# Reordering a layer norm, attention and gMLP kernel on one core: roots moved from GpSimd to ScalarE, v weights read strided, q/k before z2

## The chip, the cores and the metric

The kernel runs on one core of a Trainium2 chip. The metric is device time in microseconds (us), the median of several executions. The engines are named as the profile names them: PE (TensorE matmul; PEld is its weight load), DVE (VectorE), ACT (ScalarE), POOL (GpSimd), SP (SyncE, which issues most of the DMAs).

## The reference, cut to what matters

```python
xn = layernorm(x)                                  # x: 2048 x 512, bf16
# A: local attention, 32 heads of 16, window of 8 keys at distance 0, 2, .., 14
q, k, v = heads(xn @ wqkv)
o = softmax(q . k[t - 2w] * 16**-0.5) applied to v[t - 2w];  A = o @ wo
# B: gMLP
z = gelu(xn @ w_in)                                # 2048 x 1376, halves z1 and z2
g = w_sp @ layernorm(z2) + b_sp                    # 2048 x 2048 times 2048 x 688
B = (z1 * g) @ w_out
out = x + A + B
```

## The kernel before

The 16 row tiles of 128 are handled in four blocks of four tiles: block j holds tiles j, 4+j, 8+j, 12+j. Every tile is normalised on DVE, transposed (blocks 0 and 1 by PE and a ScalarE copy, blocks 2 and 3 by a DMA that transposes), and then used as one side of all projections. The q/k products (a shifted elementwise multiply on DVE, 1.15 us for each 128x2048) feed `logits`, a matmul that sums over a head's 16 dimensions. After that come the gate matmuls `g_mm` (w_sp times z2), which need every z2 tile.

In two waits of the kernel before's trace the engine did not pass over the instruction that had to wait. DVE stands idle for 3.06 us in front of block 3's normalisations, though the inputs of the two products written behind them were complete (ACT's copy of block 1's last q/k group ends at 32.31 us); those products start at 42.30 us. PE stands idle for 2.73 us in front of the last quarter of the first logits, with 16 q/k matmuls of block 2, whose tiles had been in use since 33.70 us, written behind it; they start at 43.95 us. The root of the layer norm is taken in three ways:

```python
def rsqrt(E, y, v, s):                 # a bit trick and three Newton steps: 15 small operations
    h, a = nwt[:, 0, s], nwt[:, 1, s]
    E.tensor_scalar(h, v, EPS, None, ALU.add)
    E.tensor_scalar(y.bitcast(I32), h.bitcast(I32), -0.5, float(0x5f3759df), ALU.mult, ALU.add)
    E.tensor_scalar(h, h, -0.5, None, ALU.mult)
    for _ in range(3):
        E.tensor_tensor(a, y, y, ALU.mult)
        E.tensor_tensor(a, a, h, ALU.mult)
        E.tensor_scalar(a, a, 1.5, None, ALU.add)
        E.tensor_tensor(y, a, y, ALU.mult)
```

Block 0 uses a ScalarE square root for each tile, block 1 and z2 use `rsqrt` on DVE, blocks 2 and 3 use `rsqrt` on GpSimd. The first part of the body, with cuts:

```python
# ... block 0: statistics, ScalarE root, normalise, transpose; z2 of two tiles as well ...
ln_block(V, 1)                         # statistics and rsqrt on DVE
for i in blk(1): ln_apply(i)
ln_block(G, 2)                         # statistics on DVE, rsqrt on GpSimd
for c in range(C):
    qk_mm(0, c)                        # ... block 1's transpositions in between
for i in blk(3): ln_stats(i)
ln_block_apply(2)                      # DVE normalises, SP issues the transposing DMA
ln_rstd(G, slice(3, NT, 4))            # rsqrt of block 3 on GpSimd
for c in range(C):
    qk_mm(1, c)
    if c == 3: ln_block_apply(3)
    prod_c(0, c); prod_c(1, c)         # DVE products of the first two groups
    if c == 1: z2s(0, 2)
for k in range(C):                     # v weights regrouped: 16 dims x 32 heads
    G.tensor_copy(wv_r[:, k], wv[:, k, :].rearrange("p (h d) -> p d h", d=DH))
qk_mm(2, 0); qk_mm(2, 1); z2s(0, 3)
logits(0)
# ... q/k of blocks 2 and 3, then z2, v and logits alternately ...
```

`v_mm` is one v group: 32 matmuls, each with a weight tile of 32 columns out of `wv_r` and a stream of 512 columns. `z2s` is one z2 tile: eight matmuls, gelu on ScalarE, and a sum of squares on ScalarE.

Of the kernel before, what the change touches and what calls it, by code (L numbers as in the profile page):

```python
# [8 lines left out]
F32 = mybir.dt.float32  # L9
# [10 lines left out]
TB = 4  # L20
# [28 lines left out]
def kernel(  # L49
# [32 lines left out]
    vp = r_x[:].rearrange("p (d t) -> p d t", d=DH)  # L82
    r_w = sb.tile([P, 8192], BF16, name="r_w")
    wqk = r_w[:, 0:4096].rearrange("p (k f) -> p k f", k=C)
    wv = r_w[:, 4096:6144].rearrange("p (k f) -> p k f", k=C)
    wv_r = r_w[:, 6144:8192].rearrange("p (k d h) -> p k d h", k=C, d=DH)
    a_sb = r_w[:, 0:4096].rearrange("p (w t) -> p w t", w=W)
    wout = r_w[:, 4096:4096 + MCH * D].rearrange("p (m n) -> p m n", m=MCH)
    r_qk = sb.tile([P, 2 * C * (HALO + S)], BF16, name="r_qk")
# [33 lines left out]
    zvar = sb.tile([P, NT], F32, name="zvar")  # L123
    zrstd = sb.tile([P, NT], F32, name="zrstd")
    eps_t = sb.tile([P, 1], F32, name="eps_t")
    nwt = sb.tile([P, 2, NT], F32, name="nwt")


    def load_x0(E, tb):
# [2 lines left out]
    def load_wqk(E, h):  # L132

        w = wqk.rearrange("p k (s c f) -> p k s c f", s=2, c=C)
        src = A_wqkv[:, 0:2 * D].rearrange("(k p) (s c f) -> p k s c f", p=P, s=2, c=C)
        for s in range(2):
            E.dma_start(w[:, :, s, 2 * h:2 * h + 2, :], src[:, :, s, 2 * h:2 * h + 2, :])
# [2 lines left out]
    load_x0(A, 2)  # L140
    load_x0(SP, 1)
    load_x0(A, 3)
    SP.dma_start(w_z2[:], B_w_in[:, FH:F].rearrange("(k p) f -> p k f", p=P))
    load_wqk(A, 0)
    SP.dma_start(xall[:, 1], xblk[1])
    load_wqk(SP, 1)
    for j in range(2, 4):
        SP.dma_start(xall[:, j], xblk[j])
    SP.dma_start(w_z1[:], B_w_in[:, 0:FH].rearrange("(k p) f -> p k f", p=P))
    SP.dma_start(wv, A_wqkv[:, 2 * D:3 * D].rearrange("(k p) f -> p k f", p=P))  # L150
    SP.dma_start(b16[:], B_b_sp.rearrange("(j p) -> j p", p=P))


# [19 lines left out]
    def ln_stats(i):  # L173
        j, tb = i % 4, i // 4
        V.bn_stats(stats[:, i, :], xall[:, j, tb, :])  # L175
        V.bn_aggr(mv[:, i, :], stats[:, i, :])  # L176

    def rsqrt(E, y, v, s):

        h, a = nwt[:, 0, s], nwt[:, 1, s]  # L180
        E.tensor_scalar(h, v, EPS, None, ALU.add)
        E.tensor_scalar(y.bitcast(I32), h.bitcast(I32), -0.5, float(0x5f3759df), ALU.mult, ALU.add)
        E.tensor_scalar(h, h, -0.5, None, ALU.mult)
        for _ in range(3):
            E.tensor_tensor(a, y, y, ALU.mult)
            E.tensor_tensor(a, a, h, ALU.mult)  # L186
            E.tensor_scalar(a, a, 1.5, None, ALU.add)  # L187
            E.tensor_tensor(y, a, y, ALU.mult)  # L188

    def ln_rstd(E, sl):  # L190
        rsqrt(E, rstd[:, sl], mv[:, sl, 1], sl)

    def ln_sqrt(i):
        A.activation(rstd[:, i:i + 1], mv[:, i:i + 1, 1], ACT.Sqrt, bias=eps_t[:])

    def ln_recip(i):
        V.reciprocal(rstd[:, i:i + 1], rstd[:, i:i + 1])

    def ln_apply(i):
        j, tb = i % 4, i // 4  # L200
        V.tensor_scalar(xall[:, j, tb, :], xall[:, j, tb, :], mv[:, i, 0:1], rstd[:, i:i + 1],  # L201
                        ALU.subtract, ALU.mult)

    def tr(i):
        j, tb = i % 4, i // 4
        pt = ps_aux.tile([P, C, P], BF16, name="pt", tag="aux")
        for c in range(C):
            PE.transpose(pt[:, c, :], xall[:, j, tb, c * P:(c + 1) * P], ident[:])
        return pt

    def tr_copy(i, pt):
        A.copy(xnT[:, :, i * P:(i + 1) * P], pt[:])

    def tr_dma(i):
        j, tb = i % 4, i // 4
        SP.dma_start_transpose(xnT[:, :, i * P:(i + 1) * P], xall[:, j, tb, :])

    def zmm(i, wz):
        pz = ps_mm.tile([P, 2, TBS], F32, name="pz", tag="mm")
        for hh in range(2):  # L220
            for kc in range(C):
                PE.matmul(pz[:, hh, 0:FHALF], xnT[:, kc, i * P:(i + 1) * P],  # L222
                          wz[:, kc, hh * FHALF:(hh + 1) * FHALF], start=(kc == 0), stop=(kc == C - 1))
        return pz
# [8 lines left out]
        junk = work.tile([P, FH], BF16, name="junk", bufs=1)  # L233
        A.activation(junk[:], z2[:, i, :], ACT.Square, accum_out=zsq[:, q:q + 1])  # L234

    def z2_stat(s):
        V.tensor_scalar(zmean[:, s], zsum[:, s], 1.0 / FH, None, ALU.mult)
        V.tensor_tensor(zm2[:, s], zmean[:, s], zmean[:, s], ALU.mult)
        V.tensor_scalar(zvar[:, s], zsq[:, s], 1.0 / FH, None, ALU.mult)
        V.tensor_tensor(zvar[:, s], zvar[:, s], zm2[:, s], ALU.subtract)  # L240
        rsqrt(V, zrstd[:, s], zvar[:, s], s)

    def z2_norm(i):
        q = 4 * (i % 4) + i // 4
        V.tensor_scalar(z2[:, i, :], z2[:, i, :], zmean[:, q:q + 1], zrstd[:, q:q + 1], ALU.subtract, ALU.mult)
# [71 lines left out]
    def v_mm(d2):  # L317
        pv = ps_mm.tile([P, 2, TBS], F32, name="pv", tag="mm")
        for dd in range(2):
            for kc in range(C):  # L320
                for tb in range(TB):
                    PE.matmul(pv[32 * tb:32 * tb + 32, dd, :], wv_r[:, kc, 2 * d2 + dd, :],  # L322
                              xnT[:, kc, tb * TBS:(tb + 1) * TBS],
                              start=(kc == 0), stop=(kc == C - 1), tile_position=(0, 32 * tb))
        A.copy(vp[:, 2 * d2:2 * d2 + 2, HALO:HALO + TBS], pv[:])
# [67 lines left out]


    pwm = ps_aux.tile([P, TBS], F32, name="pwm", tag="aux")
    for _ in range(9):
        PE.matmul(pwm[:], warm[:, 0:P], warm[:], start=True, stop=True)

    def blk(j):
        return [4 * tb + j for tb in range(TB)]  # L400

    def ln_block(E, j):
        for i in blk(j):
            ln_stats(i)
        ln_rstd(E, slice(j, NT, 4))

    def ln_block_apply(j):
        for i in blk(j):
            ln_apply(i)
            tr_dma(i)  # L410

    def z2_fin(*js):

        z2_stat(slice(4 * js[0], 4 * js[-1] + 4))
        for j in js:
            for i in blk(j):
                z2_norm(i)

    def z2s(j, tb):
        i = blk(j)[tb]  # L420
        z2_gelu(i, zmm(i, w_z2))
        z2_sq(i)

    def prods(g):
        for ww in range(4):
            prod_w(g, ww)

    t0 = blk(0)
    ln_stats(t0[0])
    ln_sqrt(t0[0])  # L430
    ln_stats(t0[1])
    ln_sqrt(t0[1])
    ln_recip(t0[0])
    ln_apply(t0[0])
    pt0 = tr(t0[0])
    tr_copy(t0[0], pt0)
    ln_stats(t0[2])
    ln_sqrt(t0[2])
    ln_recip(t0[1])
    ln_apply(t0[1])  # L440
    pt1 = tr(t0[1])
    tr_copy(t0[1], pt1)
    ln_stats(t0[3])
    ln_sqrt(t0[3])
    ln_recip(t0[2])
    ln_apply(t0[2])
    pz0 = zmm(t0[0], w_z2)
    pt2 = tr(t0[2])
    tr_copy(t0[2], pt2)
    ln_recip(t0[3])  # L450
    ln_apply(t0[3])
    pt3 = tr(t0[3])
    tr_copy(t0[3], pt3)
    z2_gelu(t0[0], pz0)
    z2_gelu(t0[1], zmm(t0[1], w_z2))
    z2_sq(t0[0])
    ln_block(V, 1)
    for i in blk(1):
        ln_apply(i)
    ln_block(G, 2)  # L460
    for c in range(C):
        qk_mm(0, c)
        if c == 0:
            z2_sq(t0[1])
        if c >= 2:
            for i in blk(1)[2 * c - 4:2 * c - 2]:
                tr_copy(i, tr(i))
    for i in blk(3):
        ln_stats(i)
    ln_block_apply(2)  # L470
    ln_rstd(G, slice(3, NT, 4))
    for c in range(C):
        qk_mm(1, c)
        if c == 3:
            ln_block_apply(3)
        prod_c(0, c)
        prod_c(1, c)
        if c == 1:
            z2s(0, 2)
    for k in range(C):  # L480
        G.tensor_copy(wv_r[:, k], wv[:, k, :].rearrange("p (h d) -> p d h", d=DH))
    qk_mm(2, 0)
    qk_mm(2, 1)
    z2s(0, 3)
    logits(0)
    qk_mm(2, 2)
    qk_mm(2, 3)
    prods(2)
    logits(1)
    qk_mm(3, 0)  # L490
    qk_mm(3, 1)
    prods(3)
    z2s(1, 0)
    logits(2)
    qk_mm(3, 2)
    qk_mm(3, 3)
    prods(4)
    z2s(1, 1)
    logits(3)
    G.memset(vp[0:32, :, 0:HALO], 0.0)  # L500
    v_mm(0)
    z2s(1, 2)
    v_mm(1)
    z2s(1, 3)
    prods(5)
    sm_max(0)
    logits(4)
    z2s(2, 0)
    v_mm(2)
    z2s(2, 1)  # L510
    logits(5)
    v_mm(3)
    z2s(2, 2)
    prods(6)
    prods(7)
    pb = ps_aux.tile([P, NT], BF16, name="pb", tag="aux")
    PE.transpose(pb[:], b16[:], ident[0:NT, 0:NT])
    A.copy(b_col[:], pb[:])
    z2_fin(0, 1)
    z2s(2, 3)  # L520
    v_mm(4)
    z2s(3, 0)
    logits(6)
    z2s(3, 1)
    v_mm(5)
    logits(7)
    add_mask()
    sm_max(1)
    for n in range(NWSP):
        load_wsp(n)  # L530
    z2s(3, 2)
    z2s(3, 3)
    for n in range(4):
        z1_mm(n)
    z2_fin(2, 3)
    v_mm(6)
    v_mm(7)
    SP.dma_start(vp[32:P, :, 0:HALO], vp[0:P - 32, :, TBS:TBS + HALO])
    sm_exp(0)
    sm_exp(1)  # L540
# [54 lines left out]
```

## Time and profile before

| | before |
|---|---|
| median time (225.39 to 228.09, 4 runs) | 227.78 us |
| span of the profiled run | 225.5 us |
| PE busy from 9 to 54 us (45.0 us) | 38.20 us, granted clock 0.89 |
| PE busy from 54 to 97.25 us (43.25 us) | 43.19 us |
| PE busy from 97.25 us, the first gate matmul, to 221.5 us | all 124.25 us |

Busy time by stretch in the kernel before; in each line come the stretch, its length, the busy time (and the number of instructions) of PE, PEld, DVE, ACT and POOL, the granted PE clock, the DMA share and GB/s:

```profile
9.00:54.00 45.00, 38.20 (x204) 17.92 (x204) 31.82 (x63) 25.17 (x39) 18.01 (x35) 0.89 0.33 90
54.00:97.25 43.25, 43.19 (x496) 21.60 (x495) 40.89 (x70) 35.73 (x69) 0.29 (x1) 1.00 0.30 58
97.25:221.50 124.25, 124.25 (x962) 74.55 (x960) 102.18 (x115) 29.46 (x33) 0.24 (x1) 1.00 0.60 129
```

From 54 to 221.5 us PE is busy throughout, at a granted clock of 1.00, so only less PE work or a faster PE could shorten that part. The slack that the change is after lies in the 45 us from 9 to 54: almost 7 us of idle PE, and a granted clock of 0.89.

The next lines are the PE timeline of the kernel before in that stretch (start, duration of a run of like instructions, source line; in brackets the idle time before it and what ended it). L257 is q/k, L222 z2, L288 logits, L208 a transposition:

```profile
27.65 3.62 PE L257 MATMUL pq<-xnT,r_w 128*128 128x512 bf16 x16
33.70 5.21 PE L257 MATMUL pq<-xnT,r_w 128*128 128x512 bf16 x16 [2.44 <-DMA xnT<-r_x]
38.75 1.33 PE L222 MATMUL pz<-w_z_75,xnT 128*128 128x344 bf16 x8
40.01 0.83 PE L288 MATMUL pl<-r_pr,rsel 128*32 128x512 bf16 x12
43.57 0.45 PE L288 MATMUL pl<-r_pr,rsel 128*32 128x512 bf16 x4 [2.73 <-DVE r_pr L271]
43.95 5.22 PE L257 MATMUL pq<-xnT,r_w 128*128 128x512 bf16 x16
```

PE waits 2.44 us for block 2's transposing DMA and 2.73 us for a DVE product. After each of those waits the 16 q/k matmuls take 5.2 us; the same 16 take 3.62 us at 27.65. The trace shows a half clock there. The next two lines of the kernel before give a stretch behind the first wait and the one after it (stretch, length, PE's busy time and number of matmuls, granted clock, DMA share, GB/s):

```profile
33.55:36.96 3.41, 3.26 (x8) 0.50 0.00 0
37.10:38.70 1.60, 1.60 (x9) 1.00 0.00 0
```

The q/k matmuls start 0.43 us apart in the first and 0.22 us apart in the second. Two more such stretches of 3.41 us are recorded before the gate: from 43.79 us, behind the second wait, and from 9.65 us, over z2 matmuls. So these two waits are paid for twice, once in idle time (2.44 and 2.73 us) and once in slower matmuls (5.2 us for 16 instead of 3.62).

What the waits hang on is seen on DVE and POOL. The DVE timeline of the kernel before (L201 is the normalisation, L271 the product):

```profile
26.60 1.39 DVE L201 TENSOR_SCALAR r_x<-r_x,mv,rstd 128x512 bf16<-128x512 bf16 x4 [1.21 <-POOL rstd L188]
27.90 6.89 DVE L271 TENSOR_TENSOR r_pr<-r_qk 128x2048 bf16<-128x2048 bf16 x6
37.86 4.52 DVE L201 TENSOR_SCALAR r_x<-r_x,mv,rstd 128x512 bf16<-128x512 bf16 x4 [3.06 <-POOL rstd L188]
```

The POOL timeline of the kernel before (L186 is one multiply of the Newton step, L481 the copy of the v weights):

```profile
25.74 0.21 POOL L186 TENSOR_TENSOR nwt<-nwt 128x4 f32<-128x4 f32 x1
...
27.79 7.07 POOL L186 TENSOR_TENSOR nwt<-nwt 128x4 f32<-128x4 f32 x1
...
37.75 4.48 POOL L481 COPY r_w<-r_w 128x512 bf16<-128x512 bf16 x4
```

One 128x4 multiply that takes 0.21 us at 25.74 takes 7.07 us at 27.79: it is recorded from 0.11 us before the first of the six DVE products (27.90 us) until just after the last has ended (34.86 against 34.79 us). And four normalisations that take 1.39 us at 26.60 take 4.52 us at 37.86, beside the four GpSimd copies. The two engines get in each other's way here in both directions, and both victims were what the rest waited for.

### The profile page before, as it was taken

Reading aid. Unit: us, or ns where it says so; the run is one execution under the profiler, and the core shown is the slowest. Engines: PE = TensorE matmul, PEld = TensorE weight load, DVE = VectorE, ACT = ScalarE, POOL = GpSimd, SP = SyncE. Lnnn points to the kernel's source line nnn. Section 1 sums busy time; section 2 is a strip of 40 time slices with the busy share of each in tenths; the row PEclk is TensorE's granted clock in tenths of the full one; section 3 lists DMA queues with packets and bytes.
Section 4 is the critical chain, followed back from the end, with each engine's and each line's share of the span. In section 5 each row is a group of like instructions: output and inputs, shape, how many; then the busy total and the mean of one; then the engine's idle time right before and its main releaser. Section 6 shows DMA issues by size and latency. Waiting matters only on the chain.

```text
span 225.5 us, 4086 instructions
## 1 busy us (share of the span) xinstructions
PE 210.7 (93%) x1674; PEld 115.9 (51%) x1674; DVE 181.6 (81%) x267; ACT 93.8 (42%) x147; POOL 22.1 (10%) x55
## 2 busy tenths in 40 slices
PE   7597959599999999999999999999999999999992
PEld 2354424134444545556666665466665466664440
DVE  4589794909799999999999999989999298882412
ACT  3299452446788898785233221012221012221000
POOL 6000798400000000000000000000000000000000
PEclk9889997889999999999999999999999999999999
DMA  5991040400000009999974766999871341111142
GB/s 172 332 350 53 0 93 0 93 6 0 0 3 0 3 0 174 221 169 219 224 161 99 155 129 146 191 149 243 206 158 35 77 144 37 35 38 35 49 140 93
DMA packets 63410, 24.97 MB, mean 111 GB/s; under 512 B 52848, under 2 KB 63264, under 8 KB 63264
## 3 DMA queue, kind: packets, MB, share of 16 engines
q1 hardware_dynamic: 62048, 23.93, 47.2%
q10 hardware_dynamic: 1344, 0.79, 1.2%
q8 instruction: 13, 0.21, 0.4%
q14 instruction: 5, 0.04, 0.1%
HBM read 9.98 MB, written 2.10 MB: 54 GB/s over the span
## 4 chain that ended last, share of the span: by engine, by line
PE 76%; DVE 8%; POOL 6%; DMA 4%; issue 2%; SPq 1%; DVEq 1%; ACT 0%
PE pg L357 33%; PE pz L222 14%; PE po L387 9%; PE pv L322 6%; PE po L381 6%; DMA r_x<-in_A_x_dram 4%; PE pq L257 4%; POOL nwt L186 4%; PE pl L288 3%; DVE r_x L201 3%; DVE stats L175 2%; DVE r_pr L281 1%; DVE mv L176 1%; POOL nwt L187 1%; POOL rstd L188 1%
## 5 line engine op out<-in xcount | busy, mean ns | idle before, releaser
L357 PE MATMUL pg<-z_77,r_qk 128*128 128x344 bf16 x512 | 76.9, 309 | 0.0
L357 PEld LDWEIGHTS <-r_qk 128*128 128x128 bf16 x512 | 50.0, 98 | 25.0 <-issue 0.4
L333 DVE TENSOR_TENSOR r_pr<-r_x,r_w 128x2048 bf16<-128x2048 bf16 x32 | 38.2, 1220 | 0.3
L360 ACT ACTIVATE gs<-pg,b_col 128x688 bf16<-128x688 f32 x16 | 13.3, 833 | 56.5 <-PE pg L357 56.5
L257 PE MATMUL pq<-xnT,r_w 128*128 128x512 bf16 x128 | 32.1, 409 | 4.1 <-DMA xnT<-r_x 2.4
L222 PEld LDWEIGHTS <-xnT 128*128 128x128 bf16 x256 | 24.7, 100 | 17.9 <-issue 5.2
L337 DVE TENSOR_TENSOR r_pr<-r_pr 128x2048 bf16<-128x2048 bf16 x28 | 33.8, 1219 | 0.1
L281 DVE TENSOR_TENSOR r_pr<-r_qk 128x2048 bf16<-128x2048 bf16 x24 | 27.5, 1218 | 6.8 <-ACT r_qk L261 6.8
L391 DVE TENSOR_TENSOR r_qk<-po,r_qk 128x512 bf16<-128x512 f32 x16 | 10.3, 686 | 18.2 <-PE po L387 18.2
L222 PE MATMUL pz<-w_z_75,xnT 128*128 128x344 bf16 x128 | 22.5, 323 | 1.7 <-DMA w_z_75<-in_B_w_in_dram 1.7
L257 PEld LDWEIGHTS <-r_w 128*128 128x128 bf16 x128 | 12.9, 104 | 21.6 <-issue 10.1
L261 ACT CAST r_qk<-pq 128x1024 bf16<-128x1024 f32 x16 | 16.2, 1012 | 16.4 <-PE pq L257 16.4
L387 PE MATMUL po<-r_w,uT 128*128 128x512 bf16 x96 | 21.4, 379 | 0.0
L250 ACT ACTIVATE z1u<-pz 128x688 bf16<-128x688 f32 x16 | 11.8, 742 | 21.8 <-PE pz L222 21.8
L222 PE MATMUL pz<-w_z_76,xnT 128*128 128x344 bf16 x128 | 20.8, 309 | 0.0
L387 PEld LDWEIGHTS <-uT 128*128 128x128 bf16 x96 | 9.1, 98 | 12.1 <-issue 1.7
L322 PE MATMUL pv<-xnT,r_w 128*32 128x512 bf16 x256 | 15.1, 380 | 0.0
L381 PE MATMUL po<-r_lg,r_pr 32*128 32x512 bf16 x256 | 14.5, 375 | 0.0
L175 DVE BATCH_NORM_STATS2 stats<-r_x 128x6 f32<-128x512 bf16 x16 | 10.7, 669 | 4.7 <-DMA r_x<-in_A_x_dram 4.7
L228 ACT ACTIVATE z_77<-pz 128x688 bf16<-128x688 f32 x16 | 11.9, 742 | 2.4 <-PE pz L222 2.4
L234 ACT ACTIVATE junk<-z_77 128x688 bf16<-128x688 bf16 x16 | 12.4, 778 | 0.4
L201 DVE TENSOR_SCALAR r_x<-r_x,mv,rstd 128x512 bf16<-128x512 bf16 x16 | 8.9, 604 | 4.5 <-POOL rstd L188 4.3
(77 smaller groups left out, 150.3 us busy)
## 6 DMA issues: line engine op xcount, KB each, us to landing
r_lg<-in_A_wo_dram SPq DMA_DIRECT2D x4, 512.0 KB, 9.4
r_qk<-in_A_x_dram SPq DMA_DIRECT2D x16, 128.0 KB, 2.2
out_dram<-r_qk SPq DMA_DIRECT2D x16, 128.0 KB, 1.7
r_x<-in_A_x_dram SPq DMA_DIRECT2D x3, 512.0 KB, 9.2
w_z_75<-in_B_w_in_dram SPq DMA_DIRECT2D x1, 688.0 KB, 7.2
w_z_76<-in_B_w_in_dram SPq DMA_DIRECT2D x1, 688.0 KB, 8.6
r_w<-in_B_w_out_dram SPq DMA_DIRECT2D x1, 640.0 KB, 6.6
r_w<-in_A_wqkv_dram ACTq DMA_DIRECT2D x2, 256.0 KB, 8.5
```

The source lines that it names most:

```text
L175: V.bn_stats(stats[:, i, :], xall[:, j, tb, :])
L201: V.tensor_scalar(xall[:, j, tb, :], xall[:, j, tb, :], mv[:, i, 0:1], rstd[:, i:i + 1], ALU.subtract, ALU.mult)
L222: PE.matmul(pz[:, hh, 0:FHALF], xnT[:, kc, i * P:(i + 1) * P], wz[:, kc, hh * FHALF:(hh + 1) * FHALF], start=(kc == 0), stop=(kc == C - 1))
L257: PE.matmul(pq[:, s, :], wqk[:, kc, s * D + c * P:s * D + (c + 1) * P], xnT[:, kc, :].rearrange("p (b j t) -> p b j t", b=TB, j=4)[:, :, j ...
L261: A.copy(dst[:, :, :, j, :], pq[:].rearrange("p s (b t) -> p s b t", b=TB))
L281: V.tensor_tensor(pr[g % 2][:, :, ww], q4, k4, ALU.mult)
L322: PE.matmul(pv[32 * tb:32 * tb + 32, dd, :], wv_r[:, kc, 2 * d2 + dd, :], xnT[:, kc, tb * TBS:(tb + 1) * TBS], start=(kc == 0), stop=(kc = ...
L333: V.tensor_tensor(pw_t[n], vp[:, :, off:off + P], a_sb[:, slot_w(w), ts].unsqueeze(1).broadcast_to([P, DH, P]), ALU.mult)
L337: V.tensor_tensor(pw_t[n] if dst is None else dst, pw_t[n], pw_t[m], ALU.add)
L357: PE.matmul(pg[:, hh, 0:FHALF], wsp[n % NWSP][:, k, :], z2[:, k, hh * FHALF:(hh + 1) * FHALF], start=(q == 0), stop=(q == NT - 1))
L381: PE.matmul(pos[tb], op[32 * tb:32 * tb + 32, d, o * P:(o + 1) * P], wo_r[32 * tb:32 * tb + 32, d, :], start=(d == 0), stop=False, tile_po ...
L387: PE.matmul(pos[tb], uT[:, o % 2, m, tb * P:(tb + 1) * P], wout[:, m, :], start=False, stop=(m == MCH - 1))
```

## The change

Its intent is to have PE start on q/k as soon as four tiles are ready, to have no GpSimd arithmetic in the way of DVE, and to keep PE full until the gate. The diff, cut to its core (cuts marked with `...`):

```diff
-    wv = r_w[:, 4096:6144].rearrange("p (k f) -> p k f", k=C)
-    wv_r = r_w[:, 6144:8192].rearrange("p (k d h) -> p k d h", k=C, d=DH)
+    wv = r_w[:, 4096:6144].rearrange("p (k h d) -> p k d h", k=C, d=DH)
...
-    SP.dma_start(w_z2[:], ...)
-    load_wqk(A, 0)
-    SP.dma_start(xall[:, 1], xblk[1])
+    load_wqk(SP, 0)
+    A.dma_start(xall[:, 1], xblk[1])
     load_wqk(SP, 1)
     for j in range(2, 4):
         SP.dma_start(xall[:, j], xblk[j])
+    SP.dma_start(w_z2[:], ...)
...
-    def ln_rstd(E, sl):
-        rsqrt(E, rstd[:, sl], mv[:, sl, 1], sl)
+    def ln_sqrt(sl):
+        A.activation(rstd[:, sl], mv[:, sl, 1], ACT.Sqrt, bias=eps_t[:])
+    def ln_recip(sl):
+        V.reciprocal(rstd[:, sl], rstd[:, sl])
...  (z2: Newton steps on DVE for blocks 0 and 1, a ScalarE root for blocks 2 and 3)
-                    PE.matmul(pv[32 * tb:32 * tb + 32, dd, :], wv_r[:, kc, 2 * d2 + dd, :],
+                    PE.matmul(pv[32 * tb:32 * tb + 32, dd, :], wv[:, kc, 2 * d2 + dd, :],
...  (the body, new)
+    for n in range(4):                          # block 0
+        if n < 3:
+            ln_stats(t0[n + 1]); ln_sqrt(col(t0[n + 1]))
+        ln_recip(col(t0[n])); ln_apply(t0[n]); tr_copy(t0[n], tr(t0[n]))
+        warm_up(3)                              # three matmuls on zeros
+    ln_stats_blk(1); ln_recip(blk_cols(1))      # ln_stats_blk ends with ln_sqrt
+    for i in blk(1): ln_apply(i)
+    qk_mm(0, 0); qk_mm(0, 1); qk_mm(0, 2)
+    for i in blk(1): tr_copy(i, tr(i))
+    ln_stats_blk(2)
+    qk_mm(0, 3)
+    ln_recip(blk_cols(2))
+    for i in blk(2): ln_apply(i); tr_dma(i)
+    qk_mm(1, 0)
+    ln_stats_blk(3); prod_c(0, 0); ln_recip(blk_cols(3))
+    for i in blk(3): ln_apply(i); tr_dma(i)
+    prod_c(1, 0)
+    for c in range(1, C): qk_mm(1, c); prod_c(0, c); prod_c(1, c)
+    z2s(0, 0)                                   # the first gelu
+    for c in range(C): qk_mm(2, c)
+    logits(0)
...
```

More of the change, by code (lines that the diff above doesn't have):

```diff
@@ L125 @@
     eps_t = sb.tile([P, 1], F32, name="eps_t")
-    nwt = sb.tile([P, 2, NT], F32, name="nwt")
     def load_x0(E, tb):
@@ L142 @@
     load_x0(A, 3)
-    SP.dma_start(w_z2[:], B_w_in[:, FH:F].rearrange("(k p) f -> p k f", p=P))
-    load_wqk(A, 0)
-    SP.dma_start(xall[:, 1], xblk[1])
+    load_wqk(SP, 0)
+    A.dma_start(xall[:, 1], xblk[1])
     load_wqk(SP, 1)
@@ L148 @@
         SP.dma_start(xall[:, j], xblk[j])
+    SP.dma_start(w_z2[:], B_w_in[:, FH:F].rearrange("(k p) f -> p k f", p=P))
+    SP.dma_start(r_w[:, 4096:6144].rearrange("p (k f) -> p k f", k=C),
+                 A_wqkv[:, 2 * D:3 * D].rearrange("(k p) f -> p k f", p=P))
     SP.dma_start(w_z1[:], B_w_in[:, 0:FH].rearrange("(k p) f -> p k f", p=P))
-    SP.dma_start(wv, A_wqkv[:, 2 * D:3 * D].rearrange("(k p) f -> p k f", p=P))
     SP.dma_start(b16[:], B_b_sp.rearrange("(j p) -> j p", p=P))
@@ L176, in ln_stats @@
         V.bn_aggr(mv[:, i, :], stats[:, i, :])
-    def rsqrt(E, y, v, s):
-        h, a = nwt[:, 0, s], nwt[:, 1, s]
-        E.tensor_scalar(h, v, EPS, None, ALU.add)
-        E.tensor_scalar(y.bitcast(I32), h.bitcast(I32), -0.5, float(0x5f3759df), ALU.mult, ALU.add)
-        E.tensor_scalar(h, h, -0.5, None, ALU.mult)
-        for _ in range(3):
-            E.tensor_tensor(a, y, y, ALU.mult)
-            E.tensor_tensor(a, a, h, ALU.mult)
-            E.tensor_scalar(a, a, 1.5, None, ALU.add)
-            E.tensor_tensor(y, a, y, ALU.mult)
-    def ln_rstd(E, sl):
-        rsqrt(E, rstd[:, sl], mv[:, sl, 1], sl)
-    def ln_sqrt(i):
-        A.activation(rstd[:, i:i + 1], mv[:, i:i + 1, 1], ACT.Sqrt, bias=eps_t[:])
-    def ln_recip(i):
-        V.reciprocal(rstd[:, i:i + 1], rstd[:, i:i + 1])
+    def ln_sqrt(sl):
+        A.activation(rstd[:, sl], mv[:, sl, 1], ACT.Sqrt, bias=eps_t[:])
+    def ln_recip(sl):
+        V.reciprocal(rstd[:, sl], rstd[:, sl])
     def ln_apply(i):
@@ L234, in z2_sq, with z2_var @@
         A.activation(junk[:], z2[:, i, :], ACT.Square, accum_out=zsq[:, q:q + 1])
-    def z2_stat(s):
+    def z2_var(j0, j1):
+        s = slice(4 * j0, 4 * j1 + 4)
         V.tensor_scalar(zmean[:, s], zsum[:, s], 1.0 / FH, None, ALU.mult)
@@ L240, in z2_stat, with z2_norms, z2_stat_dve, z2_stat_act @@
         V.tensor_tensor(zvar[:, s], zvar[:, s], zm2[:, s], ALU.subtract)
-        rsqrt(V, zrstd[:, s], zvar[:, s], s)
+        return s
+    def z2_norms(j0, j1):
+        for j in range(j0, j1 + 1):
+            for tb in range(TB):
+                z2_norm(4 * tb + j)
+    def z2_stat_dve(j0, j1):
+        s = z2_var(j0, j1)
+        y, h, a = zrstd[:, s], zvar[:, s], zm2[:, s]
+        V.tensor_scalar(h, h, EPS, None, ALU.add)
+        V.tensor_scalar(y.bitcast(I32), h.bitcast(I32), -0.5, float(0x5f3759df), ALU.mult, ALU.add)
+        V.tensor_scalar(h, h, -0.5, None, ALU.mult)
+        for _ in range(3):
+            V.tensor_tensor(a, y, y, ALU.mult)
+            V.tensor_tensor(a, a, h, ALU.mult)
+            V.scalar_tensor_tensor(y, a, 1.5, y, ALU.add, ALU.mult)
+        z2_norms(j0, j1)
+    def z2_stat_act(j0, j1):
+        s = z2_var(j0, j1)
+        A.activation(zrstd[:, s], zvar[:, s], ACT.Sqrt, bias=eps_t[:])
+        V.reciprocal(zrstd[:, s], zrstd[:, s])
+        z2_norms(j0, j1)
     def z2_norm(i):
@@ L395, with col, blk_cols, ln_stats_blk @@
     pwm = ps_aux.tile([P, TBS], F32, name="pwm", tag="aux")
-    for _ in range(9):
-        PE.matmul(pwm[:], warm[:, 0:P], warm[:], start=True, stop=True)
     def blk(j):
         return [4 * tb + j for tb in range(TB)]
-    def ln_block(E, j):
+    def col(i):
+        return slice(i, i + 1)
+    def blk_cols(j):
+        return slice(j, NT, 4)
+    def ln_stats_blk(j):
         for i in blk(j):
             ln_stats(i)
-        ln_rstd(E, slice(j, NT, 4))
-    def ln_block_apply(j):
-        for i in blk(j):
-            ln_apply(i)
-            tr_dma(i)
-    def z2_fin(*js):
-        z2_stat(slice(4 * js[0], 4 * js[-1] + 4))
-        for j in js:
-            for i in blk(j):
-                z2_norm(i)
+        ln_sqrt(blk_cols(j))
     def z2s(j, tb):
@@ L426, in prods, with warm_up @@
             prod_w(g, ww)
+    def warm_up(n):
+        for _ in range(n):
+            PE.matmul(pwm[:], warm[:, 0:P], warm[:], start=True, stop=True)
     t0 = blk(0)
+    warm_up(9)
     ln_stats(t0[0])
-    ln_sqrt(t0[0])
-    ln_stats(t0[1])
-    ln_sqrt(t0[1])
-    ln_recip(t0[0])
-    ln_apply(t0[0])
-    pt0 = tr(t0[0])
-    tr_copy(t0[0], pt0)
-    ln_stats(t0[2])
-    ln_sqrt(t0[2])
-    ln_recip(t0[1])
-    ln_apply(t0[1])
-    pt1 = tr(t0[1])
-    tr_copy(t0[1], pt1)
-    ln_stats(t0[3])
@@ L444 @@
-    ln_sqrt(t0[3])
-    ln_recip(t0[2])
-    ln_apply(t0[2])
-    pz0 = zmm(t0[0], w_z2)
-    pt2 = tr(t0[2])
-    tr_copy(t0[2], pt2)
-    ln_recip(t0[3])
-    ln_apply(t0[3])
-    pt3 = tr(t0[3])
-    tr_copy(t0[3], pt3)
-    z2_gelu(t0[0], pz0)
-    z2_gelu(t0[1], zmm(t0[1], w_z2))
-    z2_sq(t0[0])
-    ln_block(V, 1)
+    ln_sqrt(col(t0[0]))
+    for n in range(4):
+        if n < 3:
+            ln_stats(t0[n + 1])
+            ln_sqrt(col(t0[n + 1]))
+        ln_recip(col(t0[n]))
+        ln_apply(t0[n])
+        tr_copy(t0[n], tr(t0[n]))
+        warm_up(3)
@@ L458 @@
+    ln_stats_blk(1)
+    ln_recip(blk_cols(1))
     for i in blk(1):
         ln_apply(i)
-    ln_block(G, 2)
-    for c in range(C):
-        qk_mm(0, c)
-        if c == 0:
-            z2_sq(t0[1])
-        if c >= 2:
-            for i in blk(1)[2 * c - 4:2 * c - 2]:
-                tr_copy(i, tr(i))
+    qk_mm(0, 0)
+    qk_mm(0, 1)
+    qk_mm(0, 2)
+    for i in blk(1):
+        tr_copy(i, tr(i))
+    ln_stats_blk(2)
+    qk_mm(0, 3)
+    ln_recip(blk_cols(2))
+    for i in blk(2):
+        ln_apply(i)
+        tr_dma(i)
@@ L468 @@
+    qk_mm(1, 0)
+    ln_stats_blk(3)
+    prod_c(0, 0)
+    ln_recip(blk_cols(3))
     for i in blk(3):
-        ln_stats(i)
-    ln_block_apply(2)
-    ln_rstd(G, slice(3, NT, 4))
-    for c in range(C):
+        ln_apply(i)
+        tr_dma(i)
+    prod_c(1, 0)
+    for c in range(1, C):
         qk_mm(1, c)
-        if c == 3:
-            ln_block_apply(3)
         prod_c(0, c)
         prod_c(1, c)
-        if c == 1:
-            z2s(0, 2)
-    for k in range(C):
-        G.tensor_copy(wv_r[:, k], wv[:, k, :].rearrange("p (h d) -> p d h", d=DH))
@@ L482 @@
-    qk_mm(2, 0)
-    qk_mm(2, 1)
-    z2s(0, 3)
-    logits(0)
-    qk_mm(2, 2)
-    qk_mm(2, 3)
-    prods(2)
-    logits(1)
-    qk_mm(3, 0)
-    qk_mm(3, 1)
-    prods(3)
+    z2s(0, 0)
+    for c in range(C):
+        qk_mm(2, c)
+    logits(0)
+    z2s(0, 1)
+    logits(1)
+    prods(2)
+    prods(3)
+    qk_mm(3, 0)
+    z2s(0, 2)
+    qk_mm(3, 1)
+    qk_mm(3, 2)
+    z2s(0, 3)
+    logits(2)
+    qk_mm(3, 3)
     z2s(1, 0)
-    logits(2)
-    qk_mm(3, 2)
-    qk_mm(3, 3)
     prods(4)
+    logits(3)
@@ L498 @@
+    prods(5)
+    sm_max(0)
     z2s(1, 1)
-    logits(3)
-    G.memset(vp[0:32, :, 0:HALO], 0.0)
     v_mm(0)
     z2s(1, 2)
+    logits(4)
+    prods(6)
+    G.memset(vp[0:32, :, 0:HALO], 0.0)
+    z2s(1, 3)
     v_mm(1)
-    z2s(1, 3)
-    prods(5)
-    sm_max(0)
-    logits(4)
     z2s(2, 0)
+    logits(5)
+    prods(7)
+    z2s(2, 1)
     v_mm(2)
-    z2s(2, 1)
-    logits(5)
-    v_mm(3)
+    for n in range(4):
+        z1_mm(n)
     z2s(2, 2)
-    prods(6)
-    prods(7)
+    logits(6)
+    z2_stat_dve(0, 1)
@@ L516 @@
+    z2s(2, 3)
     pb = ps_aux.tile([P, NT], BF16, name="pb", tag="aux")
@@ L518 @@
     A.copy(b_col[:], pb[:])
-    z2_fin(0, 1)
-    z2s(2, 3)
-    v_mm(4)
+    v_mm(3)
     z2s(3, 0)
-    logits(6)
-    z2s(3, 1)
-    v_mm(5)
     logits(7)
@@ L528 @@
     sm_max(1)
+    z2s(3, 1)
+    z2s(3, 2)
     for n in range(NWSP):
         load_wsp(n)
-    z2s(3, 2)
     z2s(3, 3)
-    for n in range(4):
-        z1_mm(n)
-    z2_fin(2, 3)
-    v_mm(6)
-    v_mm(7)
+    v_mm(4)
+    z2_stat_act(2, 3)
+    for d2 in range(5, 8):
+        v_mm(d2)
     SP.dma_start(vp[32:P, :, 0:HALO], vp[0:P - 32, :, TBS:TBS + HALO])
```

## The prediction

> **What bounds the kernel now.** Time by stretch (busy time of each engine, cut into windows): in 97.2 to 221.5 us PE is busy all 124.3 us; in 54 to 97.2 it is busy 43.1 of 43.2 us; in 9 to 54 only 38.2 of 45 us, at a granted clock of 0.89. The chain of waits is almost pure PE from 53 us on; before, it runs through the input DMA (9.2 us, landing 11.4), layer norm statistics on DVE, some 15 us of GpSimd root arithmetic, then DVE. The timeline shows two collisions: one GpSimd multiply of 128x4 took 7.07 us instead of 0.21 while DVE ran six 2048-wide products (27.9 to 34.8), and four DVE normalisations took 4.52 us instead of 1.38 while GpSimd copied v weights (4.48 us). [...] PE pays by waits (1.7, 1.6, 2.4, 2.7 us) and by clock: 16 q/k matmuls took 5.2 us after two of those waits, 3.5 us otherwise.
>
> **What the change does.** GpSimd roots become a ScalarE root of 0.30 us and a DVE reciprocal of 0.17; block 1's DVE root chain (about 2.9 us) goes. The extra table load (1.28 us), for the z2 root of blocks 2 and 3, runs beside v matmuls. q/k weights load before z2 weights, so q/k can start after four tiles. PE work is the same, plus warm-up matmuls inside waits.
>
> **Ledger.** Trace durations (q/k 1.73 us each x16, z2 1.22 x16, logits 0.98 x8, v 1.78 x8, four z1 at 1.17, DVE products 1.15 each x32, statistics 0.79, normalisations 0.35, transposing DMA 1.2 issue and 2.4 to landing), walked in the new order by engine: q/k starts at about 11 us, behind the fourth tile's copy and warm-ups, then PE waits little over 1 us in all. Products of the last group end near 74 us (83.5 now), so w_sp loads start earlier and don't bind. The z2 normalisation ends about 2 us into the gate matmuls, whose third block is read about 2.3 us in: tight, harmless. First gate matmul at about 88 us instead of 97.2: 9.2 us gained. After it PE is saturated in the same order; softmax and apply shift equally, so the gain stays.
>
> **Doubt on v weights.** They now lie 32 bytes apart. [...] v matmuls come every 56 ns now, their 32-column weight loads hidden. If a strided load takes longer than 56 ns, all 8 v groups grow, on the critical path. I book 0.5 us, with a tail of 6.
>
> **Time.** 227.8 - 9.2 + 0.5, plus some 0.5 for stalls that I missed: 219.5 us, range 215.5 to 224. Chances: faster by over 2% 0.83, within 2% 0.14, slower 0.03.
>
> **Right if:** no GpSimd work between 6 and 40 us; normalisations of block 3 at about 0.35 us each; q/k matmuls x16 always near 3.5 us; first gate matmul at 86 to 90 us; PE still fully busy after it; v group 1.8 us. **Wrong if:** v group above 2 us (strided reads); q/k weights land after 11 us; PE waits for products or transposing DMAs in 25 to 60 us; the roots stand behind q/k copies on ScalarE and block 2's transposes come late; DVE backlog makes output matmuls wait.

227.8 - 9.2 + 0.5 + 0.5 is 219.6 us. But the doubt about the v weights rested on one of the cut sentences: its 0.5 us, and its tail of 6, are the author's allowance and come from no measured number. That loads of more than 56 ns would make the groups grow was an estimate from the pace of the v matmuls (1.78 us for 32), and the runs don't bear it out (runs 9 and 10).

## The result, and the profile after

| | before | after |
|---|---|---|
| median time | 227.78 us | 217.94 us (217.84 to 219.06, 4 runs) |
| ratio after / before, 95% interval | | 0.9601 (0.9529 to 0.9673) |
| span of the profiled run | 225.5 us | 216.0 us |
| start of the first gate matmul | 97.25 us | 87.87 us |

Ratios here and below are formed from mean times of fast runs of the same rounds, so they are not quite the ratio of the medians quoted.

Busy time by stretch in the changed kernel, same columns as before:

```profile
9.00:54.00 45.00, 43.70 (x298) 20.93 (x297) 36.28 (x59) 33.09 (x55) 0.77 (x2) 1.00 0.33 93
54.00:87.87 33.87, 33.87 (x402) 19.64 (x401) 31.19 (x56) 30.15 (x58) 0.00 (x0) 1.00 0.46 81
87.87:212.00 124.13, 123.60 (x956) 74.60 (x960) 99.55 (x104) 29.45 (x33) 0.00 (x0) 1.00 0.63 127
```

In 9 to 54 us PE is now idle for 1.3 us instead of 6.8, at a granted clock of 1.00, and does 298 matmuls there instead of 204. From 9 us to the gate PE's idle time falls from 6.86 to 1.30 us, and its busy time from 81.39 to 77.57 us, with 700 matmuls recorded in either kernel: 5.56 and 3.82 us make up the 9.38 us by which the gate comes earlier. The second part fits the clock, since the changed kernel's trace records no half-clock stretch before the gate; the mix of matmuls differs a little (warm-ups, transpositions), so this is an account and not an experiment. The stretch after the first gate matmul has its old length: 124.13 us, against 124.25. (The half microsecond by which PE is not busy in it stems from a few matmuls whose records are missing in this trace: the output group has 92 of its 96.)

The PE timeline of the changed kernel (L267 is q/k, L192 a transposition, L298 logits):

```profile
10.47 5.34 PE L267 MATMUL pq<-xnT,r_w 128*128 128x512 bf16 x24
...
17.40 0.87 PE L192 MATMUL pt<-ident,r_x 128*128 128x128 bf16 x8 [1.14 <-DVE mv L175]
18.11 8.80 PE L267 MATMUL pq<-xnT,r_w 128*128 128x512 bf16 x40
...
27.91 7.07 PE L267 MATMUL pq<-xnT,r_w 128*128 128x512 bf16 x32
34.91 1.05 PE L298 MATMUL pl<-r_pr,rsel 128*32 128x512 bf16 x16
```

One wait of 1.14 us is left, between the transpositions of block 1. The profile names a statistics operation on DVE, which ended just before but which a transposition does not use; the traces of runs 2, 3, 6 and 7 name the ScalarE copy of the transposed tiles for the same wait. The q/k matmuls keep one pace (24 in 5.34 us, 32 in 7.07, 40 in 8.80). DVE in the changed kernel (L185 is the normalisation of blocks 2 and 3; the four of block 3 are back at 1.39 us, against 4.52):

```profile
19.35 1.38 DVE L185 TENSOR_SCALAR r_x<-r_x,mv,rstd 128x512 bf16<-128x512 bf16 x4
...
25.17 1.39 DVE L185 TENSOR_SCALAR r_x<-r_x,mv,rstd 128x512 bf16<-128x512 bf16 x4
26.47 8.04 DVE L281 TENSOR_TENSOR r_pr<-r_qk 128x2048 bf16<-128x2048 bf16 x7
```

### The profile page after: what moved, and what is told of

It is laid out like the page before. It is cut to its first block, busy times and chain, and to the rows that moved or that the text cites. A ratio compares the mean times of both kernels' runs of the same rounds, so it can differ in the third digit from the quotient of the medians.

```text
span 216.0 us, 4048 instructions
## 1 busy us (share of the span) xinstructions
PE 207.4 (96%) x1682; PEld 117.6 (54%) x1686; DVE 173.9 (80%) x238; ACT 96.3 (45%) x152; POOL 4.3 (2%) x21
## 4 chain that ended last, share of the span: by engine, by line
PE 93%; DVE 2%; DMA 1%; ACT 1%; DVEq 1%; issue 0%
PE pg L367 35%; PE pz L206 18%; PE pq L267 13%; PE po L397 10%; PE pv L332 7%; PE po L391 7%; PE pl L298 4%; DMA r_x<-in_A_x_dram 1%; DVE stats L174 1%; PE pwm L432 1%; DVE r_x L185 1%; PE pt L192 1%; DVEq L581 1%; ACT r_qk L271 0%; ACT xnT L196 0%
## 5 line engine op out<-in xcount | busy, mean ns | idle before, releaser
L206 PEld LDWEIGHTS <-xnT 128*128 128x128 bf16 x256 | 24.2, 98 | 16.2 <-issue 4.1
L267 PE MATMUL pq<-xnT,r_w 128*128 128x512 bf16 x128 | 28.6, 379 | 0.0
L397 PE MATMUL po<-r_w,uT 128*128 128x512 bf16 x92 | 20.7, 379 | 0.5 <-issue 0.5
L206 PE MATMUL pz<-w_z_75,xnT 128*128 128x344 bf16 x128 | 21.0, 310 | 0.0
L206 PE MATMUL pz<-w_z_76,xnT 128*128 128x344 bf16 x128 | 20.8, 309 | 0.0
L267 PEld LDWEIGHTS <-r_w 128*128 128x128 bf16 x128 | 12.3, 98 | 15.2 <-issue 1.2
L332 PEld LDWEIGHTS <-r_w 128*32 128x32 bf16 x256 | 9.1, 141 | 4.8 <-issue 1.1
```

Of the source, the lines that this page charges most:

```text
L206: PE.matmul(pz[:, hh, 0:FHALF], xnT[:, kc, i * P:(i + 1) * P], wz[:, kc, hh * FHALF:(hh + 1) * FHALF], start=(kc == 0), stop=(kc == C - 1))
L267: PE.matmul(pq[:, s, :], wqk[:, kc, s * D + c * P:s * D + (c + 1) * P], xnT[:, kc, :].rearrange("p (b j t) -> p b j t", b=TB, j=4)[:, :, j ...
L332: PE.matmul(pv[32 * tb:32 * tb + 32, dd, :], wv[:, kc, 2 * d2 + dd, :], xnT[:, kc, tb * TBS:(tb + 1) * TBS], start=(kc == 0), stop=(kc == ...
L397: PE.matmul(pos[tb], uT[:, o % 2, m, tb * P:(tb + 1) * P], wout[:, m, :], start=False, stop=(m == MCH - 1))
```

## The experiments

My theory 1 was that the gain comes from taking GpSimd's roots and copies off the path to the first products. The rival, theory 2, was that the order of the work makes it: q/k first, z2 later, and GpSimd is an accident. The first four runs separate them; the next four take apart the clock, the loads, the warm-ups and what was left; the last two are about the strided weights.

### 1. The old order without GpSimd work

```diff
 # kernel before
-        rsqrt(E, rstd[:, sl], mv[:, sl, 1], sl)
+        A.activation(rstd[:, sl], mv[:, sl, 1], ACT.Sqrt, bias=eps_t[:])
+        V.reciprocal(rstd[:, sl], rstd[:, sl])
 # v read strided as in the changed kernel, G.tensor_copy loop removed;
 # each root (and the normalisation after it) put behind the q/k copies that precede it on ScalarE
```

> The kernel before in its old order and with its old loads; roots of blocks 1 to 3 go to ScalarE (one extra table load there and back), each root placed after the q/k copies that precede it; v weights read strided, so no GpSimd copies. Theory 1 (what counts is that GpSimd roots and copies, and their collisions with DVE, leave the path to the first products): block 2 normalised near 23 us instead of 26.6, products of blocks 1 done near 38 us instead of 44.6, the PE waits at 31 and 41 us and the cold-clock q/k groups after them gone: 218 to 221 us, most of the 9.7 us gain. Theory 2 (the gain is the new order: q/k first, z2 after, a dense PE queue): 224 us or more.

Measured: 221.77 us (220.29 to 222.38), ratio 0.9751. That is between the two theories, outside the 218 to 221 us of theory 1. The wait for block 2's DMA is gone, the logits' wait has fallen from 2.73 to 0.84 us, and the first gate matmul starts at 90.31 us. But the ScalarE timeline of this run shows what the old order still charges: its two early gelus stand before block 1's root, so that a table load of 1.28 us stands in between; the root starts 1.30 us after that load began (L235 is the sum of squares, L191 the root):

```profile
14.70 0.78 ACT L235 ACTIVATE junk<-z 128x688 bf16<-128x688 bf16 x1
15.36 0.20 ACT L235 ACTIVATION_READ_ACCUMULATOR junk<-z 128x1 f32 x1
15.58 1.28 ACT L191 ACT_TABLE_LOAD   x1
16.88 0.30 ACT L191 ACTIVATE rstd<-mv,eps_t 128x4 f32<-128x4 f32 x1
```

The statistics were ready at 14.2 us; the root starts at 16.88. In the changed kernel there is no gelu before the last of these roots, and the roots of blocks 1 to 3 start 0.04, 1.44 and 0.04 us after their statistics. Two more things in this run should be known: block 3's normalisation stands ahead of the second pair of products, not the fourth as in the kernel before; and the start is as cold as there, since the 16 early z2 matmuls take 1.83 and 2.12 us for eight, at a granted clock of 0.50 for 3.41 us from 9.24, against 1.33 us later.

### 2. The new order with GpSimd roots

```diff
 # changed kernel, in ln_stats_blk
-        ln_sqrt(blk_cols(j))
+        if j == 1:
+            ln_sqrt(blk_cols(j))
+        else:
+            rsqrt(G, rstd[:, blk_cols(j)], mv[:, blk_cols(j), 1], blk_cols(j))
```

(The two `ln_recip` of blocks 2 and 3 go with it.)

> The changed kernel, with the roots of blocks 2 and 3 computed on GpSimd again (15 small operations each); no copies, v strided. Theory 1: block 2 normalised some 2.4 us later, block 3 and the products some 5 us later, so logits of the first group find PE waiting about 3 to 4 us near 35 us, and a cold clock after it: 221 to 223 us. Theory 2: the order hides it, within 1 us of 217.9.

Measured: 222.58 us (222.54 to 223.11), ratio 0.9783, within what theory 1 expected and far from theory 2. DVE stands idle for 4.39 and 4.14 us in front of the normalisations of blocks 2 and 3. The first of them in the DVE timeline of this run:

```profile
21.85 1.38 DVE L198 TENSOR_SCALAR r_x<-r_x,mv,rstd 128x512 bf16<-128x512 bf16 x4 [4.39 <-POOL rstd L188]
```

This is not the collision. Beside block 3's root DVE runs a single product, and one GpSimd operation is drawn out by it; the others of that root keep their 0.20 to 0.23 us. That one in the POOL timeline:

```profile
26.51 1.11 POOL L181 TENSOR_SCALAR nwt<-mv 128x4 f32<-128x4 f32 x1 [4.71 <-DVE mv L176]
```

So what costs the time here is mainly the length of the root itself, 15 GpSimd operations one after the other (17.55 to 21.81 us for block 2). PE collects three waits. The PE timeline of this run (L280 is q/k, L311 logits):

```profile
28.98 5.34 PE L280 MATMUL pq<-xnT,r_w 128*128 128x512 bf16 x24 [0.70 <-DMA xnT<-r_x]
35.35 1.89 PE L280 MATMUL pq<-xnT,r_w 128*128 128x512 bf16 x8 [1.04 <-ACT r_qk L284]
...
39.92 0.40 PE L311 MATMUL pl<-r_pr,rsel 128*32 128x512 bf16 x4 [1.87 <-DVE r_pr L294]
```

0.70, 1.04 and 1.87 us are 3.6 us of waits; the first gate matmul starts 4.36 us later than in the changed kernel (92.23 against 87.87 us).

### 3. The new order with the GpSimd copy

```diff
 # changed kernel
-                    PE.matmul(pv[...], wv[:, kc, 2 * d2 + dd, :],
+                    PE.matmul(pv[...], wv_r[:, kc, 2 * d2 + dd, :],
 ...
+    for k in range(C):
+        G.tensor_copy(wv_r[:, k], wv[:, k, :].rearrange("p (h d) -> p d h", d=DH))
     z2s(0, 0)
```

> The changed kernel with the GpSimd copy of the v weights put back and v read contiguous. Theory 1: the copies start when the v weights land (18 to 20 us), meet DVE normalisations of block 2 or 3, which take about 4.5 us instead of 1.4; products come 3 us later and PE waits 1 to 2 us: 219 to 220 us. Theory 2: within 0.7 us of 217.9. On the strided read: v groups at 1.77 us each in both, if strided loads are hidden; v weight loads back at about 97 ns from 141.

Measured: 218.04 us (217.90 to 218.07), ratio 0.9577. Theory 1 missed here: the copy costs nothing in this order. The collision is there all the same. The copy in the POOL timeline of this run:

```profile
17.83 4.38 POOL L475 COPY r_w<-r_w 128x512 bf16<-128x512 bf16 x4 [13.18 <-DMA r_w<-in_A_wqkv_dram]
```

The DVE timeline of this run, with the normalisations of block 2 and the products:

```profile
19.48 3.21 DVE L186 TENSOR_SCALAR r_x<-r_x,mv,rstd 128x512 bf16<-128x512 bf16 x4
...
28.42 8.03 DVE L282 TENSOR_TENSOR r_pr<-r_qk 128x2048 bf16<-128x2048 bf16 x7
```

The four normalisations take 3.21 us instead of 1.38, and DVE runs about 2 us late from there on (products from 28.42 us instead of 26.47). PE's logits start at 35.33 us without a wait, since PE has q/k of block 2 to do until then. The same collision was on the critical path in the old order; see the next run.

### 4. The old order with strided v alone

```diff
 # kernel before
-    for k in range(C):
-        G.tensor_copy(wv_r[:, k], wv[:, k, :].rearrange("p (h d) -> p d h", d=DH))
 ...
-                    PE.matmul(pv[...], wv_r[:, kc, 2 * d2 + dd, :],
+                    PE.matmul(pv[...], wv[:, kc, :].rearrange("p (h d) -> p d h", d=DH)[:, 2 * d2 + dd, :],
```

> The kernel before with one edit: v read strided, no GpSimd copies; GpSimd roots stay. Theory 1: block 3 normalisations at 1.4 us instead of 4.52, first logits' wait of 2.7 us gone or nearly so: 223 to 225.5 us. Theory 2: 227 to 228 us. If strided weight loads cost anything, v groups would be above 1.85 us each, and the time would rise.

Measured: 223.41 us (222.81 to 223.84), ratio 0.9812: within theory 1's range. Removing four copies that take 4.48 us on an engine that is 10% busy is worth 4.3 us. DVE in this run:

```profile
26.65 1.38 DVE L201 TENSOR_SCALAR r_x<-r_x,mv,rstd 128x512 bf16<-128x512 bf16 x4 [1.21 <-POOL rstd L188]
...
37.92 1.38 DVE L201 TENSOR_SCALAR r_x<-r_x,mv,rstd 128x512 bf16<-128x512 bf16 x4 [3.07 <-POOL rstd L188]
```

The block 3 normalisations start at the same time as before (37.92 against 37.86 us) and take 1.38 us instead of 4.52: 3.14 us. The two PE traces show the rest: the last part of the logits, which waits for those products, starts at 40.48 us instead of 43.57, 3.09 us earlier, and the 16 q/k matmuls behind it take 3.63 us instead of 5.22. No slow group follows the waits in this run, which are 1.83 and 1.17 us long: 3.61 us for the 16 q/k matmuls behind the first, 3.63 behind the second, and a granted clock of 1.00 from 9 to 54 us. That this comes from the shorter waits, and not from the luck of one execution, is argued and not shown.

Runs 1, 2 and 4 and the changed kernel make a two-by-two table, all with v read strided. "New order" means everything else in the change: the order, the loads, the warm-ups and the z2 roots. The table is not quite clean: block 1's root is on ScalarE in the whole row of the new order, and on DVE in the first cell of the old one.

| ratio to the kernel before | GpSimd roots | ScalarE roots |
|---|---|---|
| old order | 0.9812 | 0.9751 |
| new order | 0.9783 | 0.9601 |

ScalarE roots alone give 0.6%, the new order alone 0.3%, both together 2.1%. The first two are small beside the noise (the 95% intervals of the first three cells, 0.9774 to 0.9850, 0.9706 to 0.9795 and 0.9749 to 0.9817, overlap); in medians it is 1.6 and 0.8 us against 5.5 us for both. Neither theory is right by itself: the two parts need one another.

### 5. The kernel before with its waits filled

```diff
 # kernel before; filler(n) is n matmuls on zeros into a PSUM tile of its own
+    filler(10)
     qk_mm(2, 0)
     qk_mm(2, 1)
     z2s(0, 3)
-    logits(0)
+    logits(0, fill=11)                 # 11 in front of the last quarter of these matmuls
```

> The kernel before, unchanged but for idle matmuls on zeros put into its two longest PE waits: 10 before the third block's q/k, 11 before the last quarter of the first logits. They take away no wait; they keep PE busy in it. If the clock drop after the waits costs time of its own (two q/k groups at 5.2 us instead of 3.5 us, 3.4 us in the profiled run): 224 to 225.5 us, and q/k x16 at 3.6 us in both places. If the slow groups are something else: 227 to 229 us, slightly worse than before.

Measured: 225.22 us (225.00 to 225.54), ratio 0.9900 (0.9861 to 0.9940), within the range expected of the clock. The PE timeline of this run (L404 is the filler):

```profile
31.74 2.32 PE L404 MATMUL pf<-warm 128*128 128x512 bf16 x10
33.89 3.62 PE L257 MATMUL pq<-xnT,r_w 128*128 128x512 bf16 x16
...
39.37 2.55 PE L404 MATMUL pf<-warm 128*128 128x512 bf16 x11
43.25 0.40 PE L290 MATMUL pl<-r_pr,rsel 128*32 128x512 bf16 x4 [1.33 <-DVE r_pr L271]
43.58 3.63 PE L257 MATMUL pq<-xnT,r_w 128*128 128x512 bf16 x16
```

No input arrives earlier: the third block's q/k starts at 33.89 us (33.70 in the profiled run before), the last part of the logits at 43.25 us (43.57). But both q/k groups behind them take 3.6 us instead of 5.2. So some 2.5 us of the old time by the medians (1.9 us between the two profiled runs) was not waiting, but the clock that PE lost by waiting: from 9 to 54 us the granted clock is 1.00 in this run's trace and 0.89 in the kernel before's. It is the second group that counts: what the first one lost went into the wait for the product that follows, which ends at about the same time in both traces (43.25 and 43.57 us). In the kernel before the clock falls to half (0.50) behind waits of 2.44 and 2.73 us; behind waits of 1.63 us there and of 1.83 us in run 4 the 16 q/k matmuls take 3.61 us. PE was still busy for 1.12 and 0.68 us in the 3.41 us before the two falls. What sets off the fall is not shown. The effect varies between executions: the kernel before ran at mean granted clocks from 0.969 to 0.992 and in 226.4 to 228.57 us in these rounds, the filled one at 0.992 to 0.998 and within 0.54 us.

### 6. The new order with the old loads

```diff
 # changed kernel
-    load_wqk(SP, 0)
-    A.dma_start(xall[:, 1], xblk[1])
+    SP.dma_start(w_z2[:], ...)
+    load_wqk(A, 0)
+    SP.dma_start(xall[:, 1], xblk[1])
     load_wqk(SP, 1)
 # z2 weights no longer after xall; v after z1 weights
```

> The changed kernel with the load order of before (z2 weights ahead of q/k weights, block 1 of x on the same queue after them). If the load order matters: x of block 1 lands near 11.4 us instead of 8.9, so its normalisations, the transposes and all later products come 2.5 us later: 219 to 220.5 us. If it does not: within 0.6 us of 217.9.

Measured: 218.28 us (217.92 to 219.33), ratio 0.9606. The load order doesn't matter. Block 1's statistics do start later (10.62 us instead of 8.89), but PE reaches that block's transpositions only behind 24 q/k matmuls, at 15.80 us, and by then its first tiles are normalised.

### 7. The new order without warm-ups

```diff
 # changed kernel
         tr_copy(t0[n], tr(t0[n]))
-        warm_up(3)
```

> The changed kernel without the four groups of three warm-up matmuls between the first transposes. If they hold the clock: first 24 q/k matmuls slower than 5.34 us by 1 to 3 us, 218.5 to 220.5 us. If they do nothing: 217 to 218 us (the fourth transposition then comes some 0.6 us earlier).

Measured: 219.56 us (219.31 to 220.16), ratio 0.9659: 1.6 us worse. The first q/k matmuls in this run's PE timeline:

```profile
10.41 6.87 PE L267 MATMUL pq<-xnT,r_w 128*128 128x512 bf16 x24 [0.67 <-ACT xnT L196]
```

The first 24 take 6.87 us instead of 5.34, though they start at the same time. Two stretches of them (stretch, length, PE's busy time and number of matmuls, granted clock, DMA share, GB/s):

```profile
10.50:13.00 2.50, 2.50 (x7) 1.00 1.09 351
14.00:16.50 2.50, 2.50 (x14) 1.00 1.09 364
```

At first the matmuls start 0.43 us apart, then 0.22: the two paces that the kernel before has at granted clocks of 0.50 and 1.00. The record says 1.00 for both stretches here, so it does not show this cold start; that the first ran at half clock is inferred from the pace. The DMA share is the same in both, so the loads are not what slows the first. The matmuls on zeros stood in time that PE had to wait anyhow: q/k starts at 10.47 us with them and at 10.41 without.

### 8. A better version: two gaps closed

```diff
 # changed kernel
     qk_mm(0, 1)
+    for i in blk(1)[0:2]: tr_copy(i, tr(i))
     qk_mm(0, 2)
-    for i in blk(1): tr_copy(i, tr(i))
+    for i in blk(1)[2:4]: tr_copy(i, tr(i))
 ...
 # out_mm(3) only: tiles 2 and 3 in one PSUM tile each (of the pool that held the logits),
 # and each one's addition is written right behind its own matmuls
```

> A try at a better version: the changed kernel with block 1's four transpositions split two and two around a q/k group (PE waited 1.14 us there for ScalarE copies), and the last output block's final two tiles in PSUM tiles of their own, so that the first of their two additions runs under the last matmuls. Expected: the 1.14 us wait gone or under 0.3 us, 0.6 us off the tail: 216.3 to 217.2 us, 0.7 to 1.6 us below the changed kernel.

Measured: 216.12 us (216.01 to 217.24, 6 runs), ratio 0.9515 (0.9485 to 0.9545), a little better than expected and the best time. In its PE timeline no wait is left between the transpositions (L192):

```profile
14.22 0.61 PE L192 MATMUL pt<-ident,r_x 128*128 128x128 bf16 x8
...
16.39 0.61 PE L192 MATMUL pt<-ident,r_x 128*128 128x128 bf16 x8
16.84 8.86 PE L267 MATMUL pq<-xnT,r_w 128*128 128x512 bf16 x40
```

In its DVE timeline the addition of the last tile but one runs under the last matmuls:

```profile
209.57 0.69 DVE L406 TENSOR_TENSOR r_qk<-pl,r_qk 128x512 bf16<-128x512 f32 x1
210.87 0.69 DVE L406 TENSOR_TENSOR r_qk<-pl,r_qk 128x512 bf16<-128x512 f32 x1 [0.60 <-PE pl L402]
```

In the changed kernel the last two additions (1.29 us) both came after the last matmul; here only one of 0.69 us does. 1.14 and 0.6 us account for nearly all of the 1.82 us gained.

### 9 and 10. Weight loads with a stride of 32 bytes, under half the stream

Run 3 had already compared strided and contiguous v weights. The group of v weight loads in the changed kernel, strided (line, engine, operation, tiles, shape and count; busy time and mean ns of one; idle time before):

```profile
L332 PEld LDWEIGHTS <-r_w 128*32 128x32 bf16 x256 | 9.1, 141 | 4.8 <-issue 1.1
```

The same group in run 3, contiguous:

```profile
L333 PEld LDWEIGHTS <-r_w 128*32 128x32 bf16 x256 | 6.4, 96 | 7.0 <-issue 1.1
```

A strided load is recorded with 141 ns, a contiguous one with 96 ns. The eight v groups take 14.62 us in the chain of waits strided (four of 1.89, and 7.06 for the last four) and 14.38 us contiguous (four of 1.84, and 7.02): 0.24 us in all. To see whether the load hides only because the stream is long, the changed kernel and run 3's were run with half of it:

```diff
-                    PE.matmul(pv[.., dd, :], wv[:, kc, 2 * d2 + dd, :], xnT[:, kc, 512 columns], ...)
+            for th in range(2):  (outside the kc and tb loops)
+                    PE.matmul(pv[.., dd, 256 * th:256 * th + 256], wv[:, kc, 2 * d2 + dd, :],
+                              xnT[:, kc, 256 columns], ...)
```

> The changed kernel with every v matmul cut in two halves of 256 columns, so each weight load has half the stream to hide behind (64 loads a group instead of 32, the same arithmetic). v read strided, loads 141 ns each as recorded. If the strided load is hidden only because the stream is long: v groups grow well above 1.89 us, to 2.5 us or more, and more than in the contiguous twin. If the stride costs the array nothing: the same v group time as the twin.

> Twin of half_streams_strided: the same halves, with v copied contiguous on GpSimd at the place where that copy cost nothing (218.04 us against 217.94). Expected: v groups at 1.8 to 2.2 us if a 32-column contiguous load takes less than the 28 ns that the halved stream leaves; the difference to the strided twin, over 8 groups, is the bare cost of the 32-byte stride.

Measured: 218.31 us (218.20 to 218.40) strided, 218.47 us (218.10 to 219.04) contiguous; ratios 0.9572 and 0.9585. The group of loads in the strided run:

```profile
L333 PEld LDWEIGHTS <-r_w 128*32 128x32 bf16 x512 | 13.9, 139 | 1.2 <-issue 1.1
```

The group of loads in the contiguous run:

```profile
L334 PEld LDWEIGHTS <-r_w 128*32 128x32 bf16 x512 | 13.2, 97 | 1.4 <-issue 1.1
```

With 64 loads to a group the v group takes 1.91 us strided and 1.86 us contiguous: the same 0.05 us apart as with 32. Strided or not, these loads are recorded as longer than the pace at which the matmuls come (some 55 and 28 ns, from 7.06 us for 128 and 7.14 us for 256). That alone did not make the groups grow, unlike what the forecast (56 ns) and the contiguous twin's expectation (28 ns) had estimated. I read the 0.05 us (it is an estimate from them and from 141 - 96 ns, not an experiment) as a delay of 45 ns that is seen once, where a v group begins behind other work, and that doesn't lower the rate of one load in 28 ns (the last four groups, 256 loads, take 7.14 us strided). Of the two outcomes named beforehand the second came: the strided groups did not grow to 2.5 us.

## Why the prediction was right or wrong

The prediction was right: 219.5 us (215.5 to 224) against 217.94 us. Point by point:

- **Where the time is.** The ledger put the first gate matmul at about 88 us; it starts at 87.87. q/k starts at 10.47 us (about 11 said), PE waits 1.30 us from 9 to 54 us ("little over 1"), the last products end at 72.6 us ("near 74"), the z2 normalisation ends 1.45 us after the first gate matmul starts ("about 2"). After it the time is unchanged: 124.13 us against 124.25.
- **The sum.** Of the spans of the two profiled runs, 9.38 us of the difference came from the earlier gate and 0.12 us from the stretch behind it; the medians differ by 9.84 us, 0.34 us more than these two runs do. The two surcharges were mis-sized: 0.5 us for strided loads (0.24 measured) and 0.5 us for stalls that I missed (none).
- **Strided v weights.** The doubt did not come true. A strided load is recorded as longer (141 against 96 ns; why is not shown), and PE's pace hardly depends on it here (0.05 us for a v group).
- **No GpSimd work from 6 to 40 us.** Nearly: two fills of constants remain, 0.30 and 0.52 us near 32 us, and the trace shows nothing that waits for them.
- **Causes that the prediction credited wrongly.** It listed "q/k weights load before z2 weights, so q/k can start after four tiles" as a part of the gain; with the old loads q/k starts at the same time (10.62 us) and the time is 218.28 us. It booked nothing for the warm-ups, while its ledger took every q/k group at full pace; without them the kernel is 1.6 us slower. It named the copy's collision as a cost to be removed; that is worth 4.3 us in the old order and 0.1 us in the new. And it did not see that the parts need one another: with GpSimd roots the new order gains 0.3% (0.9812 to 0.9783), with ScalarE roots 1.5% (0.9751 to 0.9601).
- **The clock.** The prediction read the slow q/k groups as a part of the loss; filling the waits showed that it is about 2.5 us of the time before.

Left open: whether the clock in run 4 stayed up because of the shorter waits; and which of three things, the table load, the early z2 tiles or the cold start, holds the old order back most once its roots are on ScalarE.

## What to carry to other kernels

Before crediting an engine swap or a reordering, test both in both states: here a fast root was worth little (0.6%) while gelu stood before it, and a dense order was worth little (0.3%) while the root was slow. An idle GpSimd (10% busy) did not make small work on it free here, where 0.21 us became 7.07: look for one of its instructions, or of DVE's, whose duration is a multiple of its twin's (4.52 against 1.38 us), and ask whether something waits for it at that moment. Where PE had to wait anyhow, matmuls on zeros kept up its pace without a cost that the traces show, and paid off in the matmuls behind the wait: 3.6 us instead of 5.2 for 16 in run 5, and 5.34 us in the changed kernel against 6.87 for 24 in run 7.
